# Strassen's algorithm in the last layer of a fused attention, expert and MLP kernel, with its activations kept in DRAM between two passes

## The chip, the cores and the metric

The kernel runs on one core of a Trainium2 chip. The metric is device microseconds (us) from the start to the end of one execution. The engines are TensorE (PE in the profile, with PEld for its weight loads), VectorE (DVE), ScalarE (ACT), GpSimd (POOL) and SyncE (SP, which issues most DMAs).

## What is computed

The reference is attention with a block mask, then a layer of experts in which each token goes to one of eight, then a two-layer perceptron. The change touches the last of these only:

```python
def _moe2_ref(x, w_in, w_out) -> np.ndarray:   # x (2304, 512), w_in (512, 2048), w_out (2048, 512)
    h = x @ w_in
    beta = 1.0
    neg = h <= -beta
    pos = h >= beta
    g = np.where(pos, h, np.where(neg, 0.0, (h + beta) ** 2 / (4.0 * beta)))
    return (g @ w_out).astype(np.float32)
```

The weights w_in and w_out come as 64-bit floats. The kernel reads them as pairs of 32-bit words and converts them on the chip.

## The kernel before

Products are made in three terms: each float32 operand is split into a high part (a copy in the type float32r, by ScalarE) and a low part (the rest, by a subtraction), and TensorE adds high x high, high x low and low x high in PSUM.

The last layer takes the 2304 tokens in six groups g of 384 (G3), which are three tiles of 128 rows, and the 2048 hidden columns in 16 tiles f of 128. `blocks` lists all 96 pairs (g, f) and `last_layer` runs through them, z being the number of the block. On TensorE, VectorE, ScalarE and SP the instructions run in the order in which the Python code issues them (manual_schedule); only GpSimd's are ordered by the framework. For a block:

- `turn_y` (in three blocks of a group, f = 9 to 11): four transposes bring a row tile of the next group into PSUM (`yt`, one buffer), and ScalarE and VectorE split it into `yhi` and `ylo`. The rows were fetched by `fetch` and scaled by `scale` on GpSimd.
- `first`: 12 matmuls of 384 columns into a PSUM tile `h` (pool psh, three buffers).
- `bend`: the activation function. VectorE limits h to -1..1 (`cl`, L1177), ScalarE squares (L1178), VectorE takes the maximum with h (`gg`, L1181); ScalarE copies the high part `gh` (L1182) and `rest` subtracts for the low part `gl` (L1188).
- `second` (L1199), two blocks later: 9 matmuls of 512 columns, g times w_out, into three PSUM accumulators of 512 columns. After the last f the sums are copied and stored by an indirect DMA to the rows given in `tabs.tab`.

Between these stand the steps of `load_wo`: a 512 KB tile of w_out is loaded and `split_f64` converts it, one step per block and tile: a Square on ScalarE (L866), two instructions on VectorE (L868, L870), two more (L872, L873), then the copy of the high part on ScalarE (L875) and the subtraction of the low part on GpSimd (L876). Three of the 16 tiles (WO0) are converted in the expert stage, 13 in the first blocks of the last layer. The 16 tiles of w_in are all converted in the expert stage, by the same function. The function `between` places these steps there.

## Time and profile before

| | |
|---|---|
| median of 3 runs | 908.04 us (906.76 to 909.43) |
| the profiled execution | 908.43 us |
| its span, first to last instruction | 906.7 us |
| mean granted clock of TensorE | 0.982 of full |
| TensorE busy | 857.4 us (95%) |
| VectorE busy | 586.2 us (65%) |
| ScalarE busy | 464.5 us (51%) |
| GpSimd busy | 285.9 us (32%) |

The median is what a change is measured by. The rows below come from the one profiled execution; times in them are us from the start of the span unless marked ns. Matmuls are pipelined: a matmul's own duration reaches over the start of the next, so the distance between starts is what one costs in a row of many. The shares are means over attention (to about 230 us), the experts (to about 477 us) and the last layer.

### The profile page before, as it was taken

The page shows a single profiled execution, that of the slowest core. Times are in us where ns is not written, and L with a number is a line of the kernel's source. Part 1 is how long each engine was busy: PE and PEld are TensorE (multiplying, and loading weights), DVE is VectorE, ACT ScalarE, POOL GpSimd, SP SyncE. Part 2 cuts the span into 40 slices and gives each one's busy share as a digit, 9 for nine tenths or more (in the row PEclk, how much of TensorE's full clock was granted, in tenths as well). Part 3 has the DMA queues.
Part 4 walks back from the last instruction along what each step waited for, and adds up shares of the span by engine and source line. Part 5 has one row for each costly group of instructions (what it writes and reads, how often), then busy time and mean ns, then how long its engine had stood idle before and what let it go on. Part 6 is the DMA issues. An engine that isn't in the chain of part 4 may idle for free. (4 is left out here: it accounts for less than half of the span.)

```text
span 906.7 us, 14691 instructions
## 1 busy us (share of the span) xinstructions
PE 857.4 (95%) x5199; PEld 735.7 (81%) x5199; DVE 586.2 (65%) x1089; ACT 464.5 (51%) x998; POOL 285.9 (32%) x296
## 2 busy tenths in 40 slices
PE   6999999989887999999998999999999999999996
PEld 4677677757676898899987888999999998998994
DVE  5777887887884899998975996343343344344331
ACT  5889888876443666666643454233233233233222
POOL 7444554454457333343211756011011011000001
PEclk7999999998999999999999999999999999999998
DMA  6343344423588988898853440010010010000000
GB/s 137 70 105 92 86 106 104 102 56 106 164 240 218 265 290 283 272 278 283 268 157 103 150 128 24 12 35 23 14 36 17 18 35 14 22 1 12 24 1 35
DMA packets 144866, 99.44 MB, mean 110 GB/s; under 512 B 72887, under 2 KB 126663, under 8 KB 144784
## 3 DMA queue, kind: packets, MB, share of 16 engines
q1 hardware_dynamic: 139664, 83.95, 32.2%
q0 software_dynamic: 5120, 14.47, 4.8%
q8 instruction: 43, 0.70, 0.3%
q14 instruction: 39, 0.32, 0.1%
HBM read 84.21 MB, written 14.44 MB: 109 GB/s over the span
## 5 line engine op out<-in xcount | busy, mean ns | idle before, releaser
L896 PE MATMUL h<-yhi,wi 128*128 128x384 f32 x768 | 215.2, 341 | 4.0 <-PEq L1153 4.0
L1199 PE MATMUL oacc<-wo,gh 128*128 128x512 f32 x576 | 180.8, 394 | 1.2 <-POOL wo L876 1.2
L1177 DVE TENSOR_SCALAR cl<-h 128x384 f32<-128x384 f32 x96 | 53.4, 556 | 174.3 <-PE h L896 165.8
L1178 ACT ACTIVATE cl<-cl,half 128x384 f32<-128x384 f32 x96 | 59.3, 617 | 198.0 <-DVE cl L1177 198.0
L896 PEld LDWEIGHTS h<-yhi,wi 128*128 128x128 f32 x768 | 141.8, 190 | 7.8 <-ACTq L1153 4.4
L896 PE MATMUL h<-ylo,wi 128*128 128x384 f32 x384 | 129.9, 338 | 0.0
L1199 PEld LDWEIGHTS oacc<-wo,gh 128*128 128x128 f32 x576 | 107.2, 188 | 20.7 <-POOL wo L876 2.7
L1199 PE MATMUL oacc<-wo,gl 128*128 128x512 f32 x288 | 114.2, 397 | 0.0
L991 DVE TENSOR_TENSOR wl<-raw,wh 128x1024 fp32r<-128x1024 f32 (+1 forms) x72 | 104.1, 1445 | 0.1
L980 ACT CAST wh<-raw 128x1024 fp32r<-128x1024 f32 (+1 forms) x80 | 80.2, 1005 | 30.3 <-PE acc L1020 21.9
L315 ACT ACTIVATE pall<-s,nmax 128x384 f32<-128x384 f32 (+2 forms) x144 | 79.2, 557 | 28.6 <-DVE nmax L309 17.3
L1182 ACT CAST gh<-gg 128x384 fp32r<-128x384 f32 x96 | 49.3, 513 | 78.5 <-DVE gg L1181 68.8
L1205 POOL DMA_INDIRECT out_dram<-o,tab x18 | 17.8, 991 | 210.5 <-ACT o L1203 207.4
L896 PE MATMUL h<-xhi,wh 128*128 128x256 f32 x288 | 82.9, 288 | 0.0
L896 PE MATMUL h<-xhi,wl 128*128 128x256 f32 x288 | 81.6, 283 | 0.8 <-DVE wl L991 0.8
L896 PE MATMUL h<-xlo,wh 128*128 128x256 f32 x288 | 81.5, 283 | 0.0
L896 PEld LDWEIGHTS h<-ylo,wi 128*128 128x128 f32 x384 | 73.0, 190 | 3.4
L1181 DVE TENSOR_TENSOR gg<-h,cl 128x384 f32<-128x384 f32 x96 | 53.4, 557 | 26.0 <-ACT cl L1178 25.1
L333 PE MATMUL pt<-ident,pall 128*128 128x128 f32 x400 | 66.0, 282 | 1.6 <-ACT pall L315 0.6
L1020 PE MATMUL acc<-wh,hh 128*128 128x512 f32 x152 | 61.7, 406 | 5.1 <-issue 5.1
L1020 PE MATMUL acc<-wh,hl 128*128 128x512 f32 x152 | 60.7, 399 | 3.4 <-DVE slot_i L835 1.7
L1199 PEld LDWEIGHTS oacc<-wo,gl 128*128 128x128 f32 x288 | 54.2, 188 | 11.7 <-DVE gl L1188 0.3
(255 smaller groups left out, 1741.7 us busy)
## 6 DMA issues: line engine op xcount, KB each, us to landing
raw<-in_moe_w_dram SPq DMA_DIRECT2D x160, 256.0 KB
wi_raw<-in_moe_w_in_dram SPq DMA_DIRECT2D x16, 512.0 KB
wo_raw<-in_moe_w_out_dram SPq DMA_DIRECT2D x16, 512.0 KB
x_dram<-xrow SPq DMA_DIRECT2D x36, 128.0 KB
yr<-y_dram SPq DMA_DIRECT2D x18, 256.0 KB
v<-in_v_dram SPq DMA_DIRECT2D x32, 128.0 KB
k<-in_k_dram SPq DMA_DIRECT2D x32, 96.0 KB
q<-in_q_dram SPq DMA_DIRECT2D x32, 96.0 KB
```

Of the source, the lines that this page charges most:

```text
L315: nc.scalar.activation(pall[n % 2][:, o:o + w], pss[:, u:u + w], AF.Exp, bias=nm[:, x:x + 1], scale=1.0, accum_out=ssum[:, b, c, x:x + 1])
L333: nc.tensor.transpose(pt[:, kk, :], pa[:, o + kk * P:o + (kk + 1) * P], ident)
L896: nc.tensor.matmul(ps, a[za], b[zb], start=(i == 0), stop=(i == n - 1))
L980: nc.scalar.copy(ws[s, f][0][:, ab], weights.raw[s, f][:, ab])
L991: nc.vector.tensor_tensor(wl, raw, wh.bitcast(F32), op=ALU.subtract)
L1020: nc.tensor.matmul(accs[s][u], a[:, us], b[:, 1, :], start=(f == 0 and i == 0), stop=(f == NF - 1 and i == 2))
L1177: nc.vector.tensor_scalar(cl, ph, -1.0, 1.0, op0=ALU.max, op1=ALU.min)
L1178: nc.scalar.activation(cl, cl, AF.Square, bias=half, scale=0.5)
L1181: nc.vector.tensor_tensor(gg, ph, cl, op=ALU.max)
L1182: nc.scalar.copy(gh, gg)
L1199: nc.tensor.matmul(accs[g][t], a[:, us], b, start=(f == 0 and i == 0), stop=(f == NF2 - 1 and i == 2))
L1205: outs.append(nc.gpsimd.indirect_dma_start(out=out[:, :], out_offset=bass.IndirectOffsetOnAxis(ap=tabs.tab[:, j, 0:1].bitcast(U32), axis=0 ...
```

## The change

The last layer becomes two passes. The first computes `first` and `bend` for all 96 blocks; g is kept in float32, and every two blocks SP stores 384 KB of it to `g_dram`. The second pass reads two row tiles at a time (1 MB each, `g_load`; nine pairs m) and multiplies them with w_out by Strassen's algorithm in Winograd's form. The two row tiles are the halves in rows, the hidden columns 0 to 1023 and 1024 to 2047 the halves in the inner dimension, the output columns 0 to 255 and 256 to 511 the halves in columns. Each pair has seven products of quarters (`PRODS`), each of 8 inner tiles (NZ) and three terms, so 24 matmuls of 256 columns.

The left operands a11, a12, s2, s1, s4, s3, a22 are made and split by `prepare`, one per product, three products ahead; s1, s4 and s3 are sums of 1024 columns on GpSimd, s2 on VectorE. `combine` adds the products out of PSUM, on VectorE but for the first copy. The right operands b11, b21, b22 and t1 to t4 are made from w_out once. For six of the eight pairs of w_out tiles (`near_pair`) this is spread over blocks 2 to 61 of the first pass, ten steps a pair, one step a block, between the Square and gg: twice load, Square, L868 and L870, L872 and L873; then two steps of differences on GpSimd (`sums`); then two steps with two copies and two subtractions each. The last two pairs (`far_load`, `far_sums`, `far_split`) are converted in the last group's blocks and split after it, since their place is that of the w_in tiles 0 and 1 until those are done (`AREA`). All 16 tiles of w_out are now converted in the last layer, and the low parts of w_out are subtracted on VectorE. The instructions of cut_f64 are those of split_f64 but for the last two.

The diff, cut to its core:

```diff
-    def split_f64(pool, hi, lo, raw, nm, wait):
...
+    def cut_f64(pool, u, raw, nm, wait, bufs=2):
...
-        nc.scalar.copy(hi, u)
-        nc.gpsimd.tensor_tensor(lo, u, hi.bitcast(F32), op=ALU.subtract)
...
-    def load_wo(pool, g, wait=0):
-        raw = pool.tile([P, 512], I64, tag="raw64", name=f"wo_raw{g}")
-        nc.sync.dma_start(out=raw, in_=w_out[g * P:(g + 1) * P, :])
-        return split_f64(pool, wo[g][0], wo[g][1], raw, f"o{g}", wait)
...
+    wo_raw, wo_left = {}, [z + i * NF2 // 2 for z in range(NF2 // 2) for i in range(2)]
+
+    def fetch_wo():
+        if wo_left:
+            g = wo_left.pop(0)
+            wo_raw[g] = tabs.cv2.tile([P, 512], I64, tag="raw64", name=f"wo_raw{g}")
+            nc.sync.dma_start(out=wo_raw[g], in_=w_out[g * P:(g + 1) * P, :])
...
+    def load_wo(g, u):
+
+        fetch_wo()
+        return cut_f64(tabs.cv2, u, wo_raw.pop(g), f"o{g}", 0, 1)
...
+    AREA = [("f", 2, 1)] + [("s", 1, 2)] * 2 + [("g", 2, 2)] * 2 + [("op", 2, 4)] * 4
...
+        for i, (tag, n, bufs) in enumerate(AREA):
+            a = res.tile([P, n, 2, ND, P], F32R, tag=tag, name=f"wi{i}", bufs=bufs)
+            wi.extend((a[:, z, 0], a[:, z, 1]) for z in range(n))
...
+        tabs.rows = pool("c_rows", 3, yctx, **right)
+        y_ps.append(pool("c_y", 1, yctx, **right))
...
-        z, n = NF * (s - 1) + f, NF2 + WO0
+        z, n = NF * (s - 1) + f, NF2
...
-            begun.append(load_wi(g) if g < NF2 else load_wo(tabs.cv, g - NF2, 2))
+            begun.append(load_wi(g))
...
+    NEAR = NZ - 2
+
+    PRODS = (("a11", "b11"), ("a12", "b21"), ("s2", "t2"), ("s1", "t1"), ("s4", "b22"), ("s3", "t3"), ("a22", "t4"))
+    BS = {b: i for i, b in enumerate(("b11", "b21", "b22", "t1", "t2", "t3", "t4"))}
...
-    def bend(g, f, ph, fill):
...
+    def bend(g, f, ph):
...
+        if f % 2 == 0:
+            pending[:] = [tabs.gp.tile([P, NG, 2, P], F32, tag="gg", name=f"gg{g}_{f}")]
+        gg = pending[0]
+        cl = tabs.gp.tile([P, G3], F32, tag="cl", name=f"cl{g}_{f}", bufs=2)
         nc.vector.tensor_scalar(cl, ph, -1.0, 1.0, op0=ALU.max, op1=ALU.min)
         nc.scalar.activation(cl, cl, AF.Square, bias=half, scale=0.5)
-        fill()
-        rest(*late_g.pop()) if late_g else None
-        nc.vector.tensor_tensor(gg, ph, cl, op=ALU.max)
-        nc.scalar.copy(gh, gg)
-        late_g.append((g, gl, gg, gh))
-        gs[g, f] = gh, gl
-
-    def rest(g, gl, gg, gh):
-        eng = nc.gpsimd if g == 0 else nc.vector
-        eng.tensor_tensor(gl, gg, gh.bitcast(F32), op=ALU.subtract)
...
-    def second(g, fs):
...
-            for f in fs:
-                gh, gl = gs[g, f]
-                wh, wl = wo[f]
-                for i, (a, b) in enumerate(((gh, wh), (gh, wl), (gl, wh))):
-                    nc.tensor.matmul(accs[g][t], a[:, us], b,
-                                     start=(f == 0 and i == 0), stop=(f == NF2 - 1 and i == 2))
...
+        yield
+        t3 = "p (j t) -> p j t"
+        nc.vector.tensor_tensor(gg[:, :, f % 2, :], ph.rearrange(t3, t=P), cl.rearrange(t3, t=P), op=ALU.max)
+        if f % 2:
+            j = g % 2 * NG
+            nc.sync.dma_start(out=g_dram[g // 2][:, j:j + NG, f - 1:f + 1, :], in_=gg)
...
+    def sums(u0, u1, dst):
+
+        h = DM // 2
+        b11, b12, b21, b22 = u0[..., :h], u0[..., h:], u1[..., :h], u1[..., h:]
+        for d, a, b in (("t1", b12, b11), ("t2", b22, "t1"), ("t4", b21, "t2"), ("t3", b22, b12)):
+            b = dst[b] if isinstance(b, str) else b
+            nc.gpsimd.tensor_tensor(dst[d], a, b, op=ALU.subtract)
+            if d in ("t2", "t3"):
+                yield
...
+    def near_pair(z):
+
+        us = [tabs.cv2.tile([P, DM], F32, tag="cu", name=f"cuo{z}_{i}", bufs=4) for i in range(2)]
+        for i in range(2):
+            yield from load_wo(z + i * NZ, us[i])
+        c = tabs.wop.tile([P, 7, 2, DM // 2], F32R, tag="wo", name=f"wo{z}", bufs=NEAR)
+        wos[z] = c
+        ts = [tabs.cv2.tile([P, 2, DM // 2], F32, tag="cu", name=f"cut{z}_{i}", bufs=4) for i in range(2)]
+        yield from sums(*us, {n: ts[i // 2][:, i % 2] for i, n in enumerate(("t1", "t2", "t3", "t4"))})
+        h = DM // 2
+        parts = [(c[:, 0:1], us[0][:, :h].unsqueeze(1)), (c[:, 1:3], us[1].rearrange("p (x d) -> p x d", x=2)),
+                 (c[:, 3:5], ts[0]), (c[:, 5:7], ts[1])]
+        for x, (d, src) in enumerate(parts):
+            nc.scalar.copy(d[:, :, 0], src)
+            nc.vector.tensor_tensor(d[:, :, 1], src, d[:, :, 0].bitcast(F32), op=ALU.subtract)
+            if x % 2:
+                yield
...
+    def far_load(i):
+        z, x = NEAR + i // 2, i % 2
+        if i == 0:
+            far["u"] = tabs.res.tile([P, 2, 2, DM], F32, tag="f", name="wo_far", bufs=1)
+        return load_wo(z + x * NZ, far["u"][:, x, i // 2, :])
...
+    def far_sums():
+        u, h = far["u"], DM // 2
+        t = tabs.res.tile([P, 4, 2, h], F32, tag="g", name="wo_far_t", bufs=2)
+        far["src"] = {n: t[:, i] for i, n in enumerate(("t1", "t2", "t3", "t4"))}
+        for _ in sums(u[:, 0], u[:, 1], far["src"]):
+            pass
+        far["src"].update(b11=u[:, 0, :, :h], b21=u[:, 1, :, :h], b22=u[:, 1, :, h:])
...
+    def far_split(n):
+        d, src = tabs.fp.tile([P, 2, 2, DM // 2], F32R, tag=n, name=f"wof_{n}"), far["src"][n]
+        far[n] = d
+        nc.scalar.copy(d[:, 0], src)
+        nc.vector.tensor_tensor(d[:, 1], src, d[:, 0].bitcast(F32), op=ALU.subtract)
...
+    def g_load(m):
+
+        for i in range(2):
+            j = 2 * m + i
+            if m % 2 == 0:
+                t = tabs.g2.tile([P, NF2, P], F32, tag="g2", name=f"g{m}_{i}", bufs=2)
+            else:
+                t = tabs.res.tile([P, NF2, P], F32, tag="g", name=f"g{m}_{i}", bufs=2)
+            nc.sync.dma_start(out=t, in_=g_dram[j // 6][:, j % 6])
+            graw[m, i] = t
...
+        def tmp(n):
+            return tabs.res.tile([P, NZ, P], F32, tag="s", name=f"{n}f_{m}", bufs=2)
+
+        def split(n, src):
+            t = ops[m, n] = tabs.res.tile([P, 2, NZ, P], F32R, tag="op", name=f"{n}_{m}", bufs=4)
+            nc.scalar.copy(t[:, 0], src)
+            nc.vector.tensor_tensor(t[:, 1], src, t[:, 0].bitcast(F32), op=ALU.subtract)
...
+        split("a11", a11)
+        s1 = tmp("s1")
+        nc.gpsimd.tensor_tensor(s1, a21, a22, op=ALU.add)
+        yield
+        split("a12", a12)
+        s2 = tmp("s2")
+        nc.vector.tensor_tensor(s2, s1, a11, op=ALU.subtract)
+        yield
+        split("s2", s2)
+        yield
+        split("s1", s1)
+        s4 = tmp("s4")
+        nc.gpsimd.tensor_tensor(s4, a12, s2, op=ALU.subtract)
+        yield
+        split("s4", s4)
+        s3 = tmp("s3")
+        nc.gpsimd.tensor_tensor(s3, a11, a21, op=ALU.subtract)
+        yield
+        split("s3", s3)
+        yield
+        split("a22", a22)
+        yield
...
+    def product(m, i, zs):
+        a, b = PRODS[i]
+        if zs[0] == 0:
+            accs[i] = tabs.psa.tile([P, DM], F32, tag="acc", name=f"p{m}_{i}")[:, :DM // 2]
+        t = ops[m, a]
+        for z in zs:
+            w = wos[z][:, BS[b]] if z < NEAR else far[b][:, :, z - NEAR]
+            for x, (hl, wl) in enumerate(((0, 0), (0, 1), (1, 0))):
+                nc.tensor.matmul(accs[i], t[:, hl, z, :], w[:, wl], start=(z == 0 and x == 0),
+                                 stop=(z == NZ - 1 and x == 2))
...
+        if i == 0:
+            nc.scalar.copy(tmp("p1"), accs[0])
...
+        if i == 1:
+            V.tensor_tensor(o0[:, :h], accs[1], sub["p1"], op=ALU.add)
+        elif i == 2:
+            V.tensor_tensor(tmp("u2"), accs[2], sub["p1"], op=ALU.add)
+        elif i == 3:
+            V.tensor_tensor(tmp("u4"), accs[3], sub["u2"], op=ALU.add)
+        elif i == 4:
+            V.tensor_tensor(o0[:, h:], accs[4], sub["u4"], op=ALU.add)
+            put(2 * m, o0)
+        elif i == 5:
+            V.tensor_tensor(tmp("u3"), accs[5], sub["u2"], op=ALU.add)
+            V.tensor_tensor(o1[:, h:], accs[3], sub["u3"], op=ALU.add)
+        elif i == 6:
+            V.tensor_tensor(o1[:, :h], accs[6], sub["u3"], op=ALU.add)
+            put(2 * m + 1, o1)
...
-        tabs.gp, cv2_p, wo_p = pool("c_g", 3), pool("c_cv", 3), pool("c_wo", 1)
...
-        lag = 2
...
+        cvx = ExitStack()
+        tabs.wop = pool("c_wo", 1)
+        tabs.cv2, tabs.gp = pool("c_cv", 2, cvx), pool("c_g", 2, cvx)
+        y_ps.append(pool("c_y2", 1, cvx))
+        fetch_wo()
+        near = itertools.chain.from_iterable(near_pair(z) for z in range(NEAR))
+        distant = itertools.chain.from_iterable(far_load(i) for i in range(4))
+        prep = None
...
+        for z in range(total):
             g, f = blocks[z]
             more_g = g + 1 < NT // G3
             if more_g and 9 <= f < 9 + NG:
                 turn_y(g + 1, f - 9)
             ph = first(g, f)
...
+            b = bend(g, f, ph)
+            next(b)
+            if g < NT // G3 - 1:
+                if z >= 2:
+                    next(near, None)
+            else:
+                if f == 0:
+                    assert next(near, 0) == 0
+                    yctx.close()
+                    tabs.g2 = pool("c_g2", 1, side="right")
+                    g_load(0)
+                    prep = prepare(0)
+                if f >= 3:
+                    next(distant, None)
+                if f in (10, 12, 14):
+                    next(prep)
+            next(b, None)
+            if f >= 3 and prep:
+                next(distant, None)
             if more_g and f == 4:
                 for t in range(NG):
                     fetch(g + 1, t)
             if more_g and 8 <= f < 8 + NG:
...
-            if lag <= z < len(blocks):
-                g, f = blocks[z - lag]
-                second(g, [f])
...
+        for _ in distant:
+            pass
+        cvx.close()
+        tabs.fp, tabs.sp, tabs.op = pool("c_far", 1), pool("c_sub", 1), pool("c_o", 3)
+        far_sums()
+        far_split("b11")
+        far_split("b21")
+        M = NJ // 2
+        product(0, 0, range(NEAR))
+        product(0, 1, range(NEAR))
+        for m in range(M):
+            for i in range(len(PRODS)):
+                product(m, i, range(NEAR if m == 0 and i < 2 else 0, NZ))
+
+                if m == 0:
+                    for n in (("t2", "t1"), ("b22", "t3"), ("t4",), (), (), (), ())[i]:
+                        far_split(n)
+                next(prep, None)
+                combine(m, i)
+                if i == (2 if m == 0 else 0) and m + 1 < M:
+                    g_load(m + 1)
+                if i == 3:
+                    assert next(prep, 0) == 0
+                    prep = prepare(m + 1) if m + 1 < M else iter(())
```

## Rows read from the trace of the kernel before

**Rows 1.** Busy time by stretch: PE, PEld, DVE, ACT, POOL, PEclk, DMA share, GB/s.

```profile
250.00:320.00 70.00, 60.66 (x403) 52.85 (x403) 50.03 (x92) 36.50 (x57) 39.39 (x35) 0.98 0.90 248
600.00:700.00 100.00, 100.00 (x512) 90.74 (x511) 39.23 (x74) 31.65 (x57) 6.88 (x8) 1.00 0.06 19
```

**Rows 2.** Timeline, one block of the last layer: start, us, engine, line.

```profile
702.28 0.33 PE L896 MATMUL h<-yhi,wi 128*128 128x384 f32 x1
...
704.39 0.63 PE L1199 MATMUL oacc<-wo,gh 128*128 128x512 f32 x2
704.58 0.56 DVE L1177 TENSOR_SCALAR cl<-h 128x384 f32<-128x384 f32 x1 [2.33 <-PE h L896]
...
705.24 0.62 ACT L1178 ACTIVATE cl<-cl,half 128x384 f32<-128x384 f32 x1 [2.43 <-DVE cl L1177]
...
705.89 0.56 DVE L1181 TENSOR_TENSOR gg<-h,cl 128x384 f32<-128x384 f32 x1 [0.28 <-ACT cl L1178]
...
706.47 0.33 PE L896 MATMUL h<-yhi,wi 128*128 128x384 f32 x1
```

**Rows 3.** Timeline of PE: the layer's first, 37th and last matmul.

```profile
481.47 0.41 PE L896 MATMUL h<-yhi,wi 128*128 128x384 f32 x1 [3.96 <-PEq L1153]
...
489.37 0.63 PE L1199 MATMUL oacc<-wo,gh 128*128 128x512 f32 x2
...
897.28 0.39 PE L1199 MATMUL oacc<-wo,gl 128*128 128x512 f32 x1
```

**Rows 4.** Timeline of ACT across a block with a transposed row tile.

```profile
589.68 0.62 ACT L1178 ACTIVATE cl<-cl,half 128x384 f32<-128x384 f32 x1 [2.38 <-DVE cl L1177]
...
594.28 0.62 ACT L1178 ACTIVATE cl<-cl,half 128x384 f32<-128x384 f32 x1 [2.16 <-DVE cl L1177]
```

**Rows 5.** Timeline of PE, expert stage: 12 matmuls of 256 columns between these.

```profile
381.92 0.28 PE L896 MATMUL h<-xhi,wh 128*128 128x256 f32 x1
...
383.35 0.40 PE L1020 MATMUL acc<-wh,hh 128*128 128x512 f32 x1
```

**Rows 6.** Timeline of DVE while w_out is converted.

```profile
507.18 0.68 DVE L868 SCALAR_TENSOR_TENSOR sqo<-sqo,wo_raw 128x512 f32<-128x512 f32 x1
...
508.31 0.55 DVE L1177 TENSOR_SCALAR cl<-h 128x384 f32<-128x384 f32 x1
...
524.14 0.69 DVE L69 TENSOR_TENSOR ylo<-yt,yhi 128x512 fp32r<-128x512 f32 x1 [1.08 <-ACT yhi L68]
524.75 0.55 DVE L1177 TENSOR_SCALAR cl<-h 128x384 f32<-128x384 f32 x1
525.22 0.68 DVE L872 SCALAR_TENSOR_TENSOR cuo<-sqo,cuo 128x512 int32<-128x512 int32 x1
...
526.54 0.55 DVE L1181 TENSOR_TENSOR gg<-h,cl 128x384 f32<-128x384 f32 x1
527.01 0.68 DVE L868 SCALAR_TENSOR_TENSOR sqo<-sqo,wo_raw 128x512 f32<-128x512 f32 x1
```

**Rows 7.** Groups by line: count, then busy us and mean ns.

```profile
L875 ACT CAST wo<-cuo 128x512 fp32r<-128x512 f32 x16 | 9.9, 617 | 1.2 <-DVE cuo L873 1.2
```

**Rows 8.** Timeline of the expert stage: subtractions alone and beside GpSimd.

```profile
379.04 1.22 DVE L991 TENSOR_TENSOR wl<-raw,wh 128x1024 fp32r<-128x1024 f32 x1
...
379.86 1.55 POOL L876 TENSOR_TENSOR wi<-cui,wi 128x512 fp32r<-128x512 f32 x1 [4.12 <-ACT wi L875]
380.25 1.03 ACT L980 CAST wh<-raw 128x1024 fp32r<-128x1024 f32 x1
380.51 1.99 DVE L991 TENSOR_TENSOR wl<-raw,wh 128x1024 fp32r<-128x1024 f32 x1
```

**Rows 9.** Timeline: a row tile's load is issued, and GpSimd scales it.

```profile
591.59 0.32 SPq L917 DMA_DIRECT2D yr<-y_dram  x1
...
594.31 0.91 POOL L924 TENSOR_SCALAR yr<-yr,tab 128x512 f32<-128x512 f32 x1 [27.67 <-DMA yr<-y_dram]
```

**Rows 10.** Busy time by stretch, as in rows 1, around one wait of PE.

```profile
520.00:525.00 5.00, 2.92 (x15) 2.18 (x14) 3.78 (x7) 2.29 (x5) 2.55 (x3) 1.00 0.38 105
525.00:530.00 5.00, 5.00 (x21) 4.66 (x22) 4.64 (x8) 2.70 (x5) 2.38 (x3) 0.66 0.34 108
```

More of the change, by code (lines that the diff above doesn't have):

```diff
@@ L80, in tile_kernel @@
     rec_dram = dram.tile([NT, 2], I32, name="rec_dram")
+    g_dram = [dram.tile([P, 6, NF2, P], F32, name=f"g_dram{i}") for i in range(NJ // 6)]
     ident = const.tile([P, P], F32, name="ident")
@@ L99, in tile_kernel @@
         overflow = experts_and_mlp(ctx, bctx, late, tc, tail, weights, w_in, w_out, x_dram, y_dram,
-                                   rec_dram, out, ident, half, tabs)
+                                   rec_dram, g_dram, out, ident, half, tabs)
     last_layer = overflow()
@@ L835, in other_slots, with experts_and_mlp @@
         V.tensor_tensor(t.slot_i[:, NSLOT:], some, nsl, op=ALU.max)
-def experts_and_mlp(ctx, bctx, late, tc, a_tail, weights, w_in, w_out, x_dram, y_dram, rec_dram, out,
+def experts_and_mlp(ctx, bctx, late, tc, a_tail, weights, w_in, w_out, x_dram, y_dram, rec_dram, g_dram, out,
                     ident, half, tabs):
@@ L1212, in last_layer @@
-    def last_layer():
-        tabs.gp, cv2_p, wo_p = pool("c_g", 3), pool("c_cv", 3), pool("c_wo", 1)
-        wo.extend([wo_p.tile([P, DM], F32R, name=f"wo{g}_{z}") for z in range(2)] for g in range(WO0, NF2))
-        y_ps.append(pool("c_y2", 1))
-        tabs.op = pool("c_o", 3)
-        lag = 2
-        conv = {x: load_wo(cv2_p, x) for x in range(WO0, WO0 + 2)}
-        for z in range(len(blocks)):
+        yield
+        t3 = "p (j t) -> p j t"
+        nc.vector.tensor_tensor(gg[:, :, f % 2, :], ph.rearrange(t3, t=P), cl.rearrange(t3, t=P), op=ALU.max)
@@ new lines, in experts_and_mlp @@
+    far = {}
+    def far_load(i):
[10 more added lines that the diff above has]
+        far["src"].update(b11=u[:, 0, :, :h], b21=u[:, 1, :, :h], b22=u[:, 1, :, h:])
@@ new lines, in prepare @@
+    def prepare(m):
+        a11, a12, a21, a22 = (graw[m, i][:, k * NZ:(k + 1) * NZ, :] for i in range(2) for k in range(2))
+        def tmp(n):
[26 more added lines that the diff above has]
+        yield
@@ new lines, in combine, with tmp @@
+    def combine(m, i):
+        V, h = nc.vector, DM // 2
+        def tmp(n):
+            sub[n] = tabs.sp.tile([P, h], F32, tag=n, name=f"{n}_{m}")
+            return sub[n]
+        if i == 0:
+            nc.scalar.copy(tmp("p1"), accs[0])
+            sub["o"] = [tabs.op.tile([P, DM], F32, tag="o", name=f"o{m}_{t}") for t in range(2)]
+        o0, o1 = sub["o"]
+        if i == 1:
[13 more added lines that the diff above has]
+            put(2 * m + 1, o1)
@@ new lines, in put @@
+    def put(j, o):
+        outs.append(nc.gpsimd.indirect_dma_start(
+            out=out[:, :],
+            out_offset=bass.IndirectOffsetOnAxis(ap=tabs.tab[:, j, 0:1].bitcast(U32), axis=0),
+            in_=o, in_offset=None))
+        for a in outs[:-1]:
+            tc.declare_no_dep(outs[-1].ins, a.ins, reason="other tokens")
+    def last_layer():
+        cvx = ExitStack()
[6 more added lines that the diff above has]
+        prep = None
+        total = len(blocks)
+        for z in range(total):
@@ L1224, in last_layer @@
             ph = first(g, f)
-            step = lambda y: next(conv.get(z + WO0 + y, iter(())), None)
-            bend(g, f, ph, lambda: step(-2))
-            for y in (-3, -1, 0):
-                step(y)
-            if z + WO0 + 2 < NF2:
-                conv[z + WO0 + 2] = load_wo(cv2_p, z + WO0 + 2)
+            b = bend(g, f, ph)
[17 more added lines that the diff above has]
+                next(distant, None)
             if more_g and f == 4:
@@ L1235, in last_layer @@
                 scale(g + 1, f - 8)
-            if lag <= z < len(blocks):
-                g, f = blocks[z - lag]
-                second(g, [f])
-        while late_g:
-            rest(*late_g.pop())
-        second(g, [NF2 - 2, NF2 - 1])
+        for _ in distant:
[21 more added lines that the diff above has]
+                    prep = prepare(m + 1) if m + 1 < M else iter(())
     return overflow
```

40 lines of the change are left out of this document (13 added, 27 removed).

## The prediction

> **What bounds the kernel now.** I read the busy shares by stretch first. In the middle of the last layer TensorE (PE) is busy for all 100 of 100 us at full clock while VectorE (DVE) works 39 and ScalarE (ACT) 32 [rows 1]: only matmuls count there. The timeline gives their price by the start-to-start distance, since their own durations overlap. The 12 matmuls of 384 columns of one block take 702.28 to 704.39, 2.11 us; the 9 of 512 columns after them take until 706.47, 2.08 us or 231 ns each; a block is 4.19 us [rows 2]. The layer's matmuls run from 481.47 to 897.67, 416.2 us [rows 3]. That is 96 blocks x 4.19 = 402.2; 15 transposed row tiles, each lengthening its block from 4.19 to 4.60, so 6.2 [rows 2, 4]; a slow beginning, where the first three blocks' 36 matmuls take 7.90 and not 6.33, so 1.6 [rows 3]; and 6.2 of waits, nearly all while w_out is still being converted.
>
> **The second product.** Removed: 96 x 9 = 864 matmuls of 512 columns, 864 x 0.231 = 199.6 us. Added: 9 pairs of row tiles x 7 products x 8 x 3 = 1512 matmuls of 256 columns. The expert stage has that size: 12 of them take 381.92 to 383.35, 119 ns each [rows 5], so 180.2 us. An eighth less arithmetic would be worth 25.0 us; 19.4 are left, because a matmul of half the columns takes 119 of 231 ns, a little over half.
>
> **The first pass: who paces it.** Without second() a block offers TensorE 2.11 us, and in these VectorE and ScalarE must finish what they had 4.19 for. VectorE runs its queue in order: cl, the conversion step of this block, gg, the next cl. From cl to gg is 1.31 us even with nothing between, since gg waits for ScalarE's Square [rows 2], and from gg to the following VectorE instruction 0.47 [rows 6]. A plain block is 1.78 us: VectorE gains 0.33 on TensorE.
>
> A pair of w_out tiles passes in ten blocks (near_pair, six pairs, from block 2 on). Four have no VectorE work: 1.78 each. Two have L868 and L870: 0.47 + 1.13 (507.18 to 508.31) + 0.47 = 2.07. Two have L872 and L873: 524.75 to 527.01, 2.26, as they stand [rows 6]. In the ninth and tenth VectorE waits in its queue for ScalarE's copies, which stand behind the Square. A copy of 512 columns is 0.62 [rows 7] and one of 1024 is 1.03 [rows 8], so one of 256 about 0.42; VectorE's two-input step is 0.68 for 512 [rows 6] and 1.22 for 1024 [rows 8], so about 0.41 for 256. Counted from cl, Square ends at 1.28, and back-to-back instructions overlap by 0.09. Ninth: copies end at 1.61 and 2.14, the second subtraction runs 2.18 to 2.86, gg from 2.78: 3.25. Tenth: copies end at 1.81 and 2.33, subtractions at 2.53 and 3.13: 3.52. The ten together are 22.55 us against TensorE's 21.10.
>
> PSUM has three buffers for h, so VectorE may fall some 2.3 us behind before TensorE waits (two blocks of 4.2 less the 1.9 from the end of a product to the end of gg). Six pairs lose 6 x 1.45 = 8.7. The four groups of three row tiles in this stretch put ylo on VectorE (0.69, its successor 0.61 later, [rows 6]) where TensorE is lengthened by 0.41 only, and the single PSUM buffer of yt makes TensorE wait for ylo before the next tile, so its lead is gone when the next heavy step comes. I followed all 96 blocks with these durations and that wait: TensorE loses 13.3 us by block 64 and nothing in blocks 65 to 79.
>
> The last sixteen blocks get two steps of the far tiles per block from f = 3 to 8, some 17.2 us of VectorE for TensorE's 12.7, so 4.5, and three steps of prepare(0), each a ScalarE copy of 1024 (1.03), then a subtraction of 1.22, the middle one with s2 as well: 1.7 + 2.9 + 1.7. Of these 10.8 the light blocks between and the buffers take back 4.2; TensorE loses 6.6. The first pass is 96 x 2.11 + 1.6 + 6.2 + 13.3 + 6.6 = 230.3.
>
> **Between the passes.** gg of the last block ends 5.2 us after TensorE; b11's subtraction follows at 5.8. TensorE has the 36 near matmuls of two products meanwhile, 4.3: it waits 1.5.
>
> **The second pass.** A pair takes TensorE 20.0 us. VectorE has seven subtractions and s2, 8 x 1.22 = 9.8, and seven sums of 256 columns out of PSUM at about 0.42 = 2.9; ScalarE 7 x 1.03. Each operand is made three products, 8.6 us, ahead. GpSimd (POOL) has three operations of 1024 columns, twice 1.55 each [rows 8], 9.3. Its work delays VectorE: the same subtraction took 1.22 us alone and 1.99 when 0.90 of it lay beside a GpSimd operation, 0.77 for 0.90, or 86% [rows 8]. If the operations meet by chance, 9.3 x 9.8 / 20.0 = 4.6 us of them do, which adds 3.9: 16.6 of 20.0. TensorE sets the pace, 180.2.
>
> The Trainium skill (SBUF — State Buffer, "SBUF: two separate sides") says that VectorE with two SBUF inputs and GpSimd hold one port pair as an exclusive lock, the loser blocked for the whole instruction. The 86% nearly bears it out; by that rule, with every GpSimd operation beside a subtraction, a pair would take VectorE 22.0 us and the pass 198, not 180.2.
>
> **The rest.** In the first pass the same delay falls on L868 to L873. GpSimd works there on the four differences of a pair, while VectorE has only cl and gg, and those read PSUM; on the row scaling, twelve tiles of 0.91 [rows 9]; and in the last group on s1 and the far differences, some 9. The bounds are 0 and 0.86 x 20 x one half, about 8.6; I take 1.6, near the low end, because in the long blocks VectorE sits waiting for ScalarE anyway. Three w_out loads leave the expert stage. Most of it has no gap on TensorE; where it has (9.3 us of 70, the transfers at 0.90), one load of 0.5 MB less is worth 0 to 2.1 at 248 GB/s [rows 1]; I take 0.5. Activations written and read, 18.9 MB each way: 384 KB per two blocks is some 90 GB/s, 2 MB per 20 us some 105, both well under 248; no cost while their latency is covered. The end keeps its shape: a combination from PSUM in place of the copy, then the same indirect store.
>
> Sum: 230.3 + 1.5 + 180.2 = 412.0 against 416.2, so -4.2; with +1.6 and -0.5, -3.1. From the profiled execution's 908.4 that gives 905.3; the median lies 0.4 below that execution, so 905.0.
>
> **Rivals.**
> First, the conversions hide and TensorE is not held. Then 20 of the 21.4 us of waits come back: 885; half of them, 895. For it: VectorE's sum of work exceeds TensorE's by only 7% over ten blocks. Against it: even at 4.19 us a block the conversion makes TensorE wait now, 2.08 us in 520 to 525 [rows 10].
>
> Second, the other side: the waits pull the clock down. After that wait the clock stood at 0.66 of full for the next 5 us [rows 10], partly at 1.2 GHz, and cost 0.34 x 5 = 1.7 us. My first pass has ten waits of 0.8 us or more, five of them over 1.5. If only those over 1.9 count, half hidden because TensorE waits anyway, it is +2; if 0.8 us suffices and each is paid in full, 10 x 1.7 = 17 at worst and about 9 with some hidden: 914. It decides from the second such payment on. For it: the row. Against it: the expert stage's stretch with 9 us of gaps kept 0.98 [rows 1].
>
> Third, VectorE paces the second pass. If every GpSimd operation met subtractions and stopped them for its whole length, a pair would be 9.8 + 2.9 + 9.3 = 22.0 us; from 20.0 on it decides, so 0 to 9 x 2.0 = 18 us. A quarter of that, +5, gives 910. For it: the 86%; against it: operations that don't meet cost nothing.
>
> Fourth, the data are late at the turn. g_load(0) puts 2 MB on SP's queue in front of the far tiles' raw data and the gg stores, at 248 GB/s 8 us; a 256 KB load alone takes 2.7 us from issue to use [rows 9]. The second far tile is wanted about 9 us after, and ScalarE and VectorE stop in order behind it: +4, 909.
>
> **How the numbers follow.** A measurement of this kernel can tell about 0.3%, 2.7 us, from no change. My forecast has 0.44 (0.31 faster, 0.13 same; its own range 900 to 909), the first rival 0.13 (faster), the second 0.22 (0.18 slower, 0.04 same), the third 0.11 (0.07, 0.04), the fourth 0.10 (0.06, 0.04). Faster 0.44, same 0.25, slower 0.31. The range 893 to 917 leaves out about half of the first rival and the worst of the second and third.
>
> **What would show it.** The first pass near 230 us with TensorE waiting for VectorE's gg around blocks 10 to 64 and 89 to 95; plain blocks at 2.11; products of 24 matmuls every 2.86 us; no wait of TensorE for op tiles in the second pass; the clock at 1.0 but for short stretches. I am wrong if TensorE's waits in the first pass are well under 15 us or over 30, if a product takes over 2.9, or if a transfer is what VectorE waits for.

## The result, and the profile after

The changed kernel took 913.02 us (median of 17 runs, 910.24 to 923.44), the kernel before beside it 908.04: a ratio of 1.0065, 95% interval 1.0044 to 1.0087. It is slower by 5 us where 3 us faster was forecast; the time is inside the range. A repetition on another occasion (E1) gave 913.75 against 904.52, ratio 1.0111 [1.0095, 1.0127]. The slowdown is 5 us in the one comparison and 9 in the other.

The first profiled execution, 923.4 us, is 10 us above the median, and its excess lies ahead of the change: its last layer starts at 492.74. In E1's profile, of a 913.1 us execution, it starts at 480.87, so the rows below are E1's. Busy time by stretch, columns as in [rows 1]:

```profile
250.00:320.00 70.00, 62.19 (x406) 54.71 (x407) 47.43 (x92) 35.38 (x57) 41.62 (x35) 0.95 0.89 243
...
600.00:700.00 100.00, 94.04 (x540) 91.11 (x539) 68.91 (x123) 35.35 (x61) 13.52 (x16) 1.00 0.43 146
```

The expert stage is much as it was. In the last layer (the second row) TensorE is no longer busy for 100 of 100 us, and VectorE went from 39 to 69. The timeline of PE gives the borders of the two passes, and the last matmul:

```profile
480.87 0.44 PE L905 MATMUL h<-yhi,wi 128*128 128x384 f32 x1 [3.62 <-ACTq L1167]
...
714.12 0.33 PE L905 MATMUL h<-yhi,wi 128*128 128x384 f32 x1
714.29 4.47 PE L1317 MATMUL p<-wo,a 128*128 128x256 f32 x36
...
901.55 0.88 PE L1317 MATMUL p<-wof_t,a 128*128 128x256 f32 x6
```

First pass 714.29 - 480.87 = 233.4 us, second 902.43 - 714.29 = 188.1, the layer 421.5. Before it was 416.2 [rows 3], so +5.3, and the layer starts 0.6 earlier. In the first profile the passes are 233.7 and 186.4, the layer 420.1. What TensorE waited for, E1's waits grouped (total us, times, longest; wof_b are the far tiles of b11, b21 and b22, s the splits of s1 to s4):

```profile
PE h L905 <- DVE gg L1204: 11.2, 11, 2.3
PE yt L946 <- DVE ylo L69: 7.3, 6, 2.3
...
PE p L1317 <- DVE s L1282: 2.8, 3, 2.2
...
PE p L1317 <- ACT wof_b L1256: 0.6, 1, 0.6
```

VectorE ends nearly every one of them, and what VectorE itself waits for is ScalarE. This is its queue in the ninth and tenth step of the first near pair, in DVE's timeline:

```profile
507.75 0.56 DVE L1200 TENSOR_SCALAR cl<-h 128x384 f32<-128x384 f32 x1 [0.53 <-PE h L905]
509.34 1.22 DVE L1233 TENSOR_TENSOR wo<-cuo,wo 128x256 fp32r<-128x256 f32 x2 [1.04 <-ACT wo L1232]
510.48 0.55 DVE L1204 TENSOR_TENSOR gg<-h,cl 128x384 f32<-128x384 f32 x1
510.94 0.68 DVE L69 TENSOR_TENSOR ylo<-yt,yhi 128x512 fp32r<-128x512 f32 x1
511.54 0.55 DVE L1200 TENSOR_SCALAR cl<-h 128x384 f32<-128x384 f32 x1
513.34 1.29 DVE L1233 TENSOR_TENSOR wo<-cut,wo 128x512 fp32r<-128x512 f32 x2 [1.25 <-ACT wo L1232]
514.55 0.55 DVE L1204 TENSOR_TENSOR gg<-h,cl 128x384 f32<-128x384 f32 x1
515.02 0.55 DVE L1200 TENSOR_SCALAR cl<-h 128x384 f32<-128x384 f32 x1
```

The tenth step is 511.54 to 515.02, 3.48 us (forecast 3.52); the ninth, without the ylo step in it, 507.75 to 510.94, 3.19 (forecast 3.25). In each, over 1 us is VectorE standing before a copy of ScalarE's while TensorE's block is 2.11.

The second pass runs at 2.88 us for 24 matmuls, 0.120 each, except in pair 0. The timeline there, POOL, DVE and PE:

```profile
723.18 2.78 POOL L1296 TENSOR_TENSOR s4f<-g,s2f 128x1024 f32<-128x1024 f32 x1 [19.59 <-DVE s L1282]
726.04 2.70 POOL L1300 TENSOR_TENSOR s3f<-g,g 128x1024 f32<-128x1024 f32 x1
...
721.88 1.23 DVE L1282 TENSOR_TENSOR s<-s1f,s 128x1024 fp32r<-128x1024 f32 x1
...
723.62 2.89 DVE L1257 TENSOR_TENSOR wof_t<-wo_far_t,wof_t 128x512 fp32r<-128x512 f32 x1
727.08 2.75 DVE L1282 TENSOR_TENSOR s<-s4f,s 128x1024 fp32r<-128x1024 f32 x1 [0.57 <-ACT s L1281]
...
729.88 3.00 PE L1317 MATMUL p<-wo,s 128*128 128x256 f32 x16 [2.19 <-DVE s L1282]
```

s4f uses a buffer of tag "s" that holds s1f until the split of s1 has read it (721.88 to 723.11), so GpSimd starts s4f at 723.18; and while GpSimd works, VectorE's subtractions take 2.89 instead of 0.68 and 2.75 instead of 1.22. TensorE stands still for 2.19 us, and the granted clock falls behind it. Behind another wait, of 2.31 us shortly before the turn, it does not. E1's timeline of PE for that wait, and the busy time by stretch, PEclk the third column from the right:

```profile
712.10 0.44 PE L905 MATMUL h<-yhi,wi 128*128 128x384 f32 x1 [2.31 <-DVE gg L1204]
```

```profile
580.00:585.00 5.00, 2.69 (x15) 2.40 (x14) 3.14 (x6) 3.13 (x8) 0.00 (x0) 0.91 0.22 76
585.00:590.00 5.00, 4.81 (x23) 4.33 (x23) 3.67 (x7) 2.14 (x4) 0.00 (x0) 0.75 0.58 175
...
710.00:715.00 5.00, 2.90 (x19) 2.90 (x19) 3.53 (x6) 1.25 (x3) 0.00 (x0) 1.00 0.06 21
715.00:720.00 5.00, 4.14 (x33) 3.74 (x31) 3.30 (x6) 2.71 (x5) 0.00 (x0) 1.00 0.17 61
...
725.00:730.00 5.00, 2.81 (x24) 2.60 (x23) 4.43 (x3) 2.79 (x4) 3.66 (x2) 1.00 0.00 2
730.00:735.00 5.00, 5.00 (x30) 5.00 (x31) 5.00 (x8) 2.52 (x3) 0.00 (x0) 0.66 0.64 229
```

### The profile page after: what moved, and what is told of

The parts are those of the page before. It is cut to its first block, busy times and chain, and to the rows that moved or that the text cites. A ratio compares the mean times of both kernels' runs of the same rounds, so it can differ in the third digit from the quotient of the medians.

```text
span 921.6 us, 16392 instructions
## 1 busy us (share of the span) xinstructions
PE 848.5 (92%) x5847; PEld 760.6 (83%) x5847; DVE 679.3 (74%) x1175; ACT 478.5 (52%) x971; POOL 337.4 (37%) x319
## 5 line engine op out<-in xcount | busy, mean ns | idle before, releaser
L905 PE MATMUL h<-yhi,wi 128*128 128x384 f32 x768 | 205.2, 342 | 15.6 <-DVE gg L1204 11.5
L1005 DVE TENSOR_TENSOR wl<-raw,wh 128x1024 fp32r<-128x1024 f32 (+1 forms) x72 | 100.0, 1389 | 0.0
L1317 PE MATMUL p<-wo,s 128*128 128x256 f32 x648 | 85.2, 286 | 2.1 <-DVE s L1282 2.1
L1317 PEld LDWEIGHTS p<-wo,s 128*128 128x128 f32 x648 | 81.5, 194 | 2.5 <-DVE s L1282 2.3
L231 POOL TENSOR_TENSOR qa<-qT,qa 64x448 fp32r<-64x448 f32 x30 | 36.8, 1226 | 80.7 <-ACT qa L230 77.0
L1317 PE MATMUL p<-wo,a 128*128 128x256 f32 x486 | 63.3, 285 | 0.0
L1034 PE MATMUL acc<-wl,hh 128*128 128x512 f32 x152 | 61.2, 403 | 0.0
L1317 PEld LDWEIGHTS p<-wo,a 128*128 128x128 f32 x486 | 61.1, 194 | 0.0
```

The costliest lines, as they stand in the source:

```text
L231: eng(n, h).tensor_tensor(qa[oh, h, :7], qT[hs], qa[hs, h, :7].bitcast(F32), op=ALU.subtract)
L905: nc.tensor.matmul(ps, a[za], b[zb], start=(i == 0), stop=(i == n - 1))
L1005: nc.vector.tensor_tensor(wl, raw, wh.bitcast(F32), op=ALU.subtract)
L1034: nc.tensor.matmul(accs[s][u], a[:, us], b[:, 1, :], start=(f == 0 and i == 0), stop=(f == NF - 1 and i == 2))
L1317: nc.tensor.matmul(accs[i], t[:, hl, z, :], w[:, wl], start=(z == 0 and x == 0), stop=(z == NZ - 1 and x == 2))
```

## The experiments

The theory: the saving of the 7 products is there, and three things take it back: VectorE's ordered queue in the first pass (the copies that the near steps await, the one PSUM buffer of yt, the crowded last group), and the late s4 of pair 0 with the clock behind it. Rivals: the clock alone, a loss in the second pass, VectorE's amount of work whatever its order, or Strassen's own additions. Passes are read from each run's profile as above; totals are medians with the ratio to the kernel before, timed beside each run. That kernel's own median was 904.5 beside E1 to E4, 904.8 beside E5 to E8 and 908.6 beside E9 to E12, so across these groups the ratios are to be compared.

**E1, the changed kernel again** (no edit).

> The changed kernel once more, unedited. Theory (VectorE's queue in the first pass, where each near step awaits ScalarE's copies, plus the start of the second pass, take back what the 7 products save): median within 3 us of 913, the last layer again 420 +- 2 us (first pass 233 to 235, second 185 to 188), so the profile's 923.4 came from a longer expert stage and not from the last layer. Rival (the last layer itself varies by several us from run to run, so that the profiled one is not typical of it): last layer at 410 to 416 in a profile nearer to the median.

913.75, passes 233.4 and 188.1. The layer repeats within 1.5 us, and the second pass ends 0.1 above the expected 188; the first profile's excess was its expert stage.

**E2, one near pair converted.**

```diff
     def near_pair(z):
+        if z:
+            wos[z] = wos[0]
+            return
...
```

> Leaves out the fetch and conversion of five of the six near pairs of w_out (all six use the first pair's quarters, so the output is not the reference's); TensorE does the same products. Theory of VectorE's queue: the first pass falls from 233.7 to about 221 (a step-by-step sum of the queue gives 220.3), total about 900 to 902. Rival that the second pass and the clock hold the loss: first pass at most 4 us shorter, total 909 to 911. If the conversions were free under the matmuls: total unchanged at 913.

902.1, ratio 0.9975 [0.9959, 0.9992]. First pass 223.7 (-9.7), second 186.4. The loads of the five pairs are gone with their conversions. The conversions aren't free; the sum of the queue overstates them by 3 us.

**E3, two passes with 8 plain products.**

```diff
-        yield from sums(*us, {n: ts[i // 2][:, i % 2] for i, n in enumerate(("t1", "t2", "t3", "t4"))})
...
+        for x in range(2):
+            nc.scalar.copy(c[:, x, 0], us[x])
+            nc.vector.tensor_tensor(c[:, x, 1], us[x], c[:, x, 0].bitcast(F32), op=ALU.subtract)
+            yield
...
+            w = wos[z][:, x] if z < NEAR else far[x][:, :, z - NEAR]
+            for k, (hl, wl) in enumerate(((0, 0), (0, 1), (1, 0))):
+                nc.tensor.matmul(accs[i], t[:, hl, z, :], w[:, wl], start=((x, z) == (0, 0) and k == 0),
+                                 stop=((x, z) == (1, NZ - 1) and k == 2))
```

> The two passes with DRAM between them, but the second product as 8 products of quarters (two of 16 blocks by N=512 for each pair of token blocks): 18 rows x 48 matmuls x 0.231 us = 199.6 us of TensorE against 63 x 2.88 = 181.4. Theory: the near conversion falls from 14 to 8 quarter-splits a pair and the first pass to about 230 (-3.5), the second pass takes about 201 (+14.5), total about 922 to 925. Rival (Strassen's additions and splits cost as much as its products save): total within 3 us of 913. Rival (the two passes by themselves are the loss): total no more than 913, with the first pass still 233.

918.1, ratio 1.0163 [1.0143, 1.0182]; passes 229.8 and 196.0. The first pass is as expected; the second is 5 us shorter than expected, as it has no wait at all and a matmul of 512 columns takes 196.0 / 864 = 0.227. The total is below the expected 922 to 925. So Strassen is worth 918.1 - 913.75 = 4.4 us as the kernel stands, from four runs of each, E3's between 914.5 and 921.2. The two profiles' layers agree with it: 7.9 in the second pass against E1, of which 3.6 go in the first.

**E4, a buffer of its own for s4.**

```diff
-        s4 = tmp("s4")
+        s4 = tabs.s4.tile([P, NZ, P], F32, tag="s4", name=f"s4f_{m}")
...
+        tabs.s4 = pool("c_s4", 1)
```

> s4 = a12 - s2 gets a buffer of its own, so that GpSimd need not wait for the split of s1 before it. Theory: the 2.1 us wait of TensorE before the fifth product of pair 0 goes, and with it the stretch at half clock after it: second pass from 186.4 to 182.5 - 184, total 909.5 to 911. Rival (GpSimd and VectorE slow each other there whatever the buffer, as the split beside the GpSimd subtraction took 2.75 us instead of 1.22): the wait only shrinks to 1 us or moves to the s3 product, gain below 1.5 us.

909.48, ratio 1.0048 [1.0029, 1.0066]. The timeline of this run, the same instructions as above:

```profile
713.51 2.38 POOL L1296 TENSOR_TENSOR s4f<-g,s2f 128x1024 f32<-128x1024 f32 x1 [8.09 <-issue]
719.12 2.42 POOL L1300 TENSOR_TENSOR s3f<-g,g 128x1024 f32<-128x1024 f32 x1 [3.23 <-DVE s L1282]
...
726.92 1.23 DVE L1282 TENSOR_TENSOR s<-s4f,s 128x1024 fp32r<-128x1024 f32 x1 [0.18 <-ACT s L1281]
...
729.33 2.32 PE L1317 MATMUL p<-wo,s 128*128 128x256 f32 x18
```

GpSimd is done by 721.5, the split of s4 takes 1.23 again, and TensorE does not wait once in the second pass: 182.0, 0.1204 for each of 1512 matmuls, a little under the range expected. The rival, that the two engines meet whatever the buffer, falls in this run; E8 comes back to it.

Not all of the 6.1 us between this pass and E1's is the buffer's. E4's first pass is 235.1, 1.7 longer than E1's: the clock fell behind the wait of 2.29 before 713.90 (0.66 from 714 to 719), where E1's stayed at 1.00 behind the like wait before 712.10. The first profile has the same slower stretch there, and like E4 no wait at the turn, where E1 has 1.0. Against the first profile's second pass, 186.4, the buffer is worth 4.4: the wait of 2.1, the clock behind it 1.7, and 0.6 more.

**E5, copies one step ahead of their subtractions.**

```diff
+        for d, src in parts[:2]:
+            nc.scalar.copy(d[:, :, 0], src)
...
+        for d, src in parts[2:]:
             nc.scalar.copy(d[:, :, 0], src)
+        for x, (d, src) in enumerate(parts):
             nc.vector.tensor_tensor(d[:, :, 1], src, d[:, :, 0].bitcast(F32), op=ALU.subtract)
```

> In a near pair ScalarE's copies of the quarters are issued one step before VectorE's subtractions that await them; as many steps, the same work. Theory (the cost of the ninth and tenth steps is VectorE standing in its queue until the copies are there): first pass from 233.5 to about 223.5 (the step-by-step sum gives 222.7), total 902 to 905. Rival (VectorE's work itself is the price, not its waits): first pass unchanged within 2 us. Rival (GpSimd's sums, now beside the subtractions and copies, slow VectorE): half the gain or less, total about 908 to 910.

903.8, ratio 0.9998 [0.9983, 1.0012]; first pass 226.2 (-7.2). The tenth step in VectorE's timeline of this run:

```profile
511.50 0.55 DVE L1200 TENSOR_SCALAR cl<-h 128x384 f32<-128x384 f32 x1
511.97 1.28 DVE L1241 TENSOR_TENSOR wo<-cut,wo 128x512 fp32r<-128x512 f32 x2
513.17 0.55 DVE L1204 TENSOR_TENSOR gg<-h,cl 128x384 f32<-128x384 f32 x1
513.63 0.55 DVE L1200 TENSOR_SCALAR cl<-h 128x384 f32<-128x384 f32 x1
```

2.13 us instead of 3.48, with the same instructions: the price was the waiting. The gain is some 70% of that expected in this pass; the total fits.

**E6, y's transposed tiles in the empty PSUM banks.**

```diff
-        pt = pst.tile([P, ND, P], F32, tag="tr", name=f"yt{g}_{t}")
+        pt = (tabs.psa.tile([P, ND, P], F32, tag="acc", name=f"yt{g}_{t}") if g else
+              pst.tile([P, ND, P], F32, tag="tr", name=f"yt{g}_{t}"))
```

> The transposed y tiles of the groups after the first go to the four PSUM banks that stand empty in the first pass, in place of the single one. Theory: TensorE's waits before the second and third transposed tile of a turn (7.3 us on the subtraction of ylo in the profile of the first repetition) shrink, but most of it comes back as waits for gg, as the queue of VectorE is still late: first pass -4 (step-by-step sum 228.2 for 232.5), total 908 to 910. Rival (the waits for ylo add up in full): -7, total 906. Rival (clock alone): no more than -2.

910.33, ratio 1.0072 [1.0049, 1.0095]; first pass 229.5 (-3.9). As expected: the 7.3 us of waits for ylo go, and 4.3 come back as waits for gg (15.5 for 11.2).

**E7, the last group eased.**

```diff
             nc.scalar.copy(t[:, 0], src)
+            if m == 0:
+                yield
...
-                if f >= 3:
+                if f >= 2:
                     next(distant, None)
-                if f in (10, 12, 14):
+                if f >= 10:
                     next(prep)
             next(b, None)
-            if f >= 3 and prep:
-                next(distant, None)
```

> In the last group of token blocks the far pairs' steps come one per block instead of two, and the copies of a11, a12 and s2 come one block before their subtractions. Theory: the waits of TensorE from the third block of the last group on (about 8 us there) go: first pass from 233.5 to 225 - 227, total 905 to 907. Rival (the work moved there is too much in any order): gain under 3 us. Rival (prepared later, pair 0 of the second pass starts late): first pass shorter but a new wait at the start of the second pass, total within 2 us of 913.

906.85, ratio 1.0022 [1.0008, 1.0037]; first pass 225.1 (-8.3), second 189.2 (+1.1). TensorE's waits at the turn are now 1.78 and 0.60, 2.4 us in all, so a part of what the second rival expects, a wait at the start of the second pass, came with the theory's gain.

**E8, all of E4 to E7**, and every second h tile in the empty PSUM banks.

```diff
-        ph = psh.tile([P, 512], F32, tag="h", name=f"h2_{g}_{f}")[:, :G3]
+        ph = (tabs.psa.tile([P, DM], F32, tag="acc", name=f"h2_{g}_{f}") if f % 2 else
+              psh.tile([P, 512], F32, tag="h", name=f"h2_{g}_{f}"))[:, :G3]
```

> s4's own buffer, copies ahead, the y tiles and half of the h tiles in the empty PSUM banks, and the eased last group together. Theory: no wait left in the first pass except its cold start and VectorE near its limit (step-by-step sum 210.1; TensorE alone 204), the second pass 182: last layer 392 to 396 and total 885 to 890, 2 % under the kernel before. Rival (VectorE's own work, 22 us a near pair against 21 of TensorE, becomes the limit): first pass 216 to 220, total 893 to 898. Rival (something else, as DMA or GpSimd, holds it): above 900.

890.03, ratio 0.9849 [0.9828, 0.987]: both kernels are beaten. In the first pass, 207.9, TensorE waits only at its start; but the second is 190.9, and the layer 398.8 instead of 392 to 396. At the turn, the timelines of PE, DVE and POOL, and the busy time:

```profile
687.28 4.47 PE L1333 MATMUL p<-wo,a 128*128 128x256 f32 x36
693.37 0.39 PE L1333 MATMUL p<-wof_b,a 128*128 128x256 f32 x1 [1.62 <-ACT wof_b L1266]
698.29 2.72 PE L1333 MATMUL p<-wof_b,a 128*128 128x256 f32 x11 [4.54 <-DVE wof_b L1267]
...
687.09 2.31 DVE L1306 TENSOR_TENSOR s2f<-s1f,g 128x1024 f32<-128x1024 f32 x1
689.32 0.55 DVE L1206 TENSOR_TENSOR gg<-h,cl 128x384 f32<-128x384 f32 x1
...
692.02 3.19 DVE L1294 TENSOR_TENSOR s<-s2f,s 128x1024 fp32r<-128x1024 f32 x1
...
695.60 3.24 DVE L1267 TENSOR_TENSOR wof_b<-wo_far,wof_b 128x512 fp32r<-128x512 f32 x2
...
688.28 2.28 POOL L1217 TENSOR_TENSOR wo_far_t<-wo_far 128x512 f32<-128x512 f32 x1
...
691.76 2.36 POOL L1312 TENSOR_TENSOR s4f<-g,s2f 128x1024 f32<-128x1024 f32 x1
695.35 2.34 POOL L1316 TENSOR_TENSOR s3f<-g,g 128x1024 f32<-128x1024 f32 x1 [1.23 <-DVE s L1294]
```

```profile
692.00:697.00 5.00, 0.39 (x1) 0.19 (x1) 5.00 (x4) 3.63 (x6) 3.77 (x2) 0.71 0.08 27
697.00:702.00 5.00, 3.71 (x17) 3.71 (x18) 5.00 (x7) 2.23 (x4) 0.69 (x1) 0.50 0.82 262
```

The same three VectorE instructions in E7, whose turn is at 706.99:

```profile
706.95 2.32 DVE L1296 TENSOR_TENSOR s2f<-s1f,g 128x1024 f32<-128x1024 f32 x1
...
711.88 1.22 DVE L1284 TENSOR_TENSOR s<-s2f,s 128x1024 fp32r<-128x1024 f32 x1
...
713.49 1.28 DVE L1257 TENSOR_TENSOR wof_b<-wo_far,wof_b 128x512 fp32r<-128x512 f32 x2
```

TensorE waits 6.2 us at the turn, with the clock at half behind it; in E7 it waited 2.4. VectorE is no further behind than in E7: it begins s2f 0.2 us ahead of the turn, in E7 0.04. What is new is GpSimd. With its own buffer s4f no longer waits for the split of s1: it runs beside the split of s2, and s3f behind it beside the split of b11 and b21. These take 3.19 and 3.24 here and 1.22 and 1.28 in E7: 3.9 us more, for 3.8 more of waiting. So E4's edit, a gain alone, seems to have cost time here; no run has E8 without it.

**E9, far pairs early.** In blocks 62 to 73 no near step is left; the far pairs are cut there.

```diff
-                    next(near, None)
+                    next(steps, None)
...
+                if 2 <= f < 6:
+                    far_move(f - 2)
+                if f == 8:
+                    far_sums()
...
```

> As the run with everything, but the two far pairs are cut in the blocks in which no near pair is left (blocks 62 to 73 of 96), kept in the near pairs' buffers, and copied by ScalarE and summed by GpSimd inside the last group. Theory (with the first pass free of waits VectorE's backlog comes out at the turn: 12.7 us of waits of TensorE for the far splits there): those waits fall to 2 us or less, first pass 207 to 209, second 182 to 185, total 878 to 882. Rival (VectorE's total work is the limit, wherever it stands): the backlog comes out elsewhere and the total stays at 888 to 891. Rival (GpSimd's sums inside the last group slow VectorE and bring the waits back there): 883 to 888.

The 12.7 us in this expectation counts each wait at the weight load and again at the matmul; on the matmuls it is 6.2. Result 883.99, ratio 0.9759 [0.9722, 0.9795]; passes 209.3 and 183.1, the layer 392.4. The wait at the turn is 1.26 (timelines of PE, DVE and POOL):

```profile
695.69 0.50 PE L1338 MATMUL p<-wof_b,a 128*128 128x256 f32 x2 [1.26 <-DVE wof_b L1272]
...
692.93 3.31 DVE L1272 TENSOR_TENSOR wof_b<-wo_far,wof_b 128x512 fp32r<-128x512 f32 x2
...
692.69 2.39 POOL L1321 TENSOR_TENSOR s3f<-g,g 128x1024 f32<-128x1024 f32 x1 [1.51 <-DVE s L1299]
```

What VectorE does meanwhile is in the busy time by stretch, with TensorE at 100 of 100:

```profile
500.00:600.00 100.00, 100.00 (x592) 99.71 (x591) 81.99 (x156) 46.63 (x84) 19.99 (x28) 1.00 0.47 153
```

The wait and the second pass are as the theory has them, the first pass just above it, the total 2 us above and so in the range of the GpSimd rival; but no wait of TensorE comes back in the last group. The wait that is left at the turn goes with GpSimd: the split of b11 and b21 is 2.0 us longer beside s3f than the 1.28 of E7. E9 moves VectorE's work and GpSimd's sums of the far pairs at once, so it does not tell which of the two was worth more.

**E10, E9 with three h buffers** (the edit of E8 on h undone).

> The same without the h tiles in the empty PSUM banks (three buffers as in the changed kernel). Theory: with the copies ahead and the last group eased VectorE is never three blocks late, so the further banks bring little: first pass 207 to 211, total within 3 us of the run with them. Rival (each near pair's 22 us of VectorE against 21 of TensorE makes TensorE wait when it may not run ahead): first pass 4 to 6 us longer, total 883 to 887.

885.52, ratio 0.9778 [0.9732, 0.9823]; first pass 208.8: the theory's case. The further banks bring nothing that could be told from zero.

**E11, plain products with the same easing** (E3 with E6, h in the empty banks, copies ahead, far pairs early, the last group eased).

> Two passes with the 8 plain products, and the same easing of the first pass (copies ahead, empty PSUM banks, far pairs early). Theory: first pass 205 to 208 as nothing but TensorE is left, second pass 196, total 890 to 895: Strassen is then worth 12 to 14 us, as TensorE's difference says, and the two passes alone already beat the kernel before by about 12. Rival (without the sums and extra splits the first pass could be freer still, or the second pass has hidden waits): 4 us or more off that.

897.74, ratio 0.9904 [0.9865, 0.9944]; passes 210.9 and 196.0. Its first pass is 3 us longer than expected and the total 3 above. Strassen is worth 897.74 - 883.99 = 13.8 us here, and the two passes with plain products are 10.8 below the kernel before.

**E12, the kernel before again.**

> The kernel before, unedited, for the length of its stages a second time. Theory: last layer 416 +- 1 us, start of the last layer within 3 us of 481.5, so that the changed kernel's slowdown lies in the last layer. Rival (the part before the last layer differs between the two kernels by several us): its start at 475 to 478.

One execution, 912.8 us: layer 484.97 to 902.06, 417.1. Both misses are small, 0.5 us or less beyond the bounds; the start of the layer moves by 3.5 us between two profiles of the same kernel, so a few us of a single profile's total say nothing of the last layer. The layer itself takes 416.2 and 417.1 in the two profiles of the kernel before, 420.1 and 421.5 in those of the changed kernel.

## Why the prediction was wrong

Its sum was -3.1 us; E1's profile gives +5.3 in the layer and -0.6 ahead of it, +4.7. Term by term:

| Term | forecast | E1 |
|---|---|---|
| blocks 0 to 2, above 3 x 2.11 | 1.6 | 1.5 |
| turns of y | 6.2 | taken as forecast |
| lost in blocks 3 to 63 | 13.3 | 15.0 |
| lost in blocks 64 to 79 | 0 | 0 |
| lost in blocks 80 to 95 | 6.6 | 8.3 |
| GpSimd beside VectorE | 1.6 | in the rows above |
| **first pass** | **231.9** | **233.4** |
| wait at the turn | 1.5 | 1.0 |
| **second pass behind it** | **180.2** | **187.2** |
| expert stage | -0.5 | -0.6 |

The losses by blocks are the distances between the first matmuls of blocks 0, 3, 64, 80 and of the second pass (480.87, 488.65, 637.26, 672.26, 714.29), less 2.11 a block and 0.41 a transposed tile. The waits listed in the trace are 18.5 us of the 23.3, a slower stretch of the clock 1.7. That the term of the expert stage fits is luck: the start of the layer differs by 3.5 us between two profiles of the kernel before, and by 12 between two of the changed kernel.

**Who paces the first pass: right,** and 1.5 us too short in size. The steps read above have the predicted length within 0.06 us, and the waits lie where they were forecast. E5, E6 and E7 removed the three causes one at a time, for 7.2, 3.9 and 8.3 us.

**The step that failed** is in "The second pass": "Each operand is made three products, 8.6 us, ahead", and "TensorE sets the pace, 180.2". That holds from pair 1 on. In pair 0 the operands are made while VectorE is still behind from the first pass and has the far splits to do, and s4f's buffer is s1f's: s4's split ended after TensorE wanted it. The waits for operands are 2.8 us, and the stretch at 0.66 costs 0.34 x 5 = 1.7. A matmul takes 0.1204 (E4) instead of 0.1192, 1.8 over the pass. That is 6.3 of the 7.0 us; the rest I can't place. E4 shows the cause: with the buffer TensorE does not wait in the second pass, which is 4.4 us shorter than in the first profile and 6.1 shorter than in E1's. That its 182.0 lies 0.3 from the forecast's 181.7 for turn and pass is luck: the 1.5 forecast at the turn is not in it, and 1.8 of slower matmuls is. I worked out the steady state and took it for all nine pairs. Without these 7.0 the profile would stand at 4.7 - 7.0 = -2.3, beside the forecast -3.1.

**The rivals.** The first (conversions hide) is wrong: E2 takes five of six conversions away and gains 9.7 us in the first pass. The second (the clock) is right in kind and small: behind the start of the layer E1 has two such stretches, one in each pass, behind waits of 2.31 and 2.19 us: (0.09 + 0.25 + 0.34) x 5 = 3.4 us in all. The rival's condition, that waits over 1.9 count, held for two of E1's three: behind the wait of 2.31 before 712.10 the clock kept 1.00, as it did behind those of 1.49 and 1.80 (535 to 550). In E6 it kept 1.00 behind 2.31 and 2.21 too, and in E3 behind 3.32 but not behind 2.96. So the length of a wait did not decide it. The third (VectorE paces the second pass) is wrong as a steady state: from 730 to 830 VectorE is busy for 72 of 100 us in E1 and 87 in E4, and TensorE did not wait from pair 1 on but for 0.6 us in E1 and not at all in E4. The delay beside GpSimd is there: E1's 54 splits from pair 1 on take 90.3 us, 25 more than at 1.21 each, or 3.1 a pair where the forecast's chance meeting gave 3.9. The rule of the Trainium skill (SBUF — State Buffer, "SBUF: two separate sides") is nearly borne out by single instructions, 0.68 stretched to 2.89 beside GpSimd's 2.78 and 2.70; the 198 us that it would give if all met is not. The fourth (data late at the turn) has one trace: ScalarE stood 2.28 us before a far tile's raw data at 686.91, inside the last group, whose waits are 1.7 us above the forecast; at the turn itself no wait of over 0.3 us of TensorE, VectorE or ScalarE ends on a transfer.

What stays open: no run isolated GpSimd's share in the first pass. E1's profile bounds it: VectorE's steps L868, L872 and L1233 run some 3 us longer there than at their usual lengths, 1.7 of it in one L872 beside s1f in the last group, for the 1.6 forecast. And the comparisons put the slowdown at 5 and at 9 us, of which the profiles show 4.7; the kernel before was not profiled beside E1.

## What to carry to other kernels

Taking matmuls away is worth their time only where the engines beside TensorE still finish in the shorter block; before such a change, follow each one's queue in order and see what it stands behind, since here the same instructions, with the copies issued one step earlier, gave 7 us back. Work out the first pass through a pipeline by itself: its buffers and its helpers' backlog are not those of the steady state. And when a wait is removed, look what starts earlier for it and what that meets (E8, where GpSimd's sums came to lie beside VectorE's splits at the turn), and move work to where the helper idles (E9): together with Strassen, 24.6 us below the kernel before.
